# Regrouping two small matrix products and their copies in a recurrent attention kernel followed by a feed-forward network

## The chip, the cores and the metric

The kernel runs on one core of a Trainium2 chip. The core has a tensor engine (PE; its weight loads are listed apart as PEld), a vector engine (DVE), a scalar engine (ACT), GpSimd (POOL) and SyncE (SP), each with its own in-order queue, an on-chip memory (SBUF), and the banks that only the tensor engine writes and that DVE and ACT read (PSUM). The metric is the device time of one execution in microseconds. The kernel before takes 617.74 us, the median of three runs (617.41 to 618.44).

## The reference

Two blocks follow each other. The first is a gated linear recurrence over 4 batches, 8 heads, 768 positions, 48 features per head; the second is a two-layer network with a per-column leaky rectifier over the 3072 tokens, from 384 to 2048 and back.

```python
f = 1.0 / (1.0 + np.exp(-f_logit))
state = np.zeros((B, H, D, D), dtype=np.float32)
for t in range(S):
    state = f[:, :, t, :, None] * state + np.einsum('bhd,bhde->bhde', k[:, :, t], v[:, :, t])
    y[:, :, t] = np.einsum('bhd,bhde->bhe', q[:, :, t], state)
...
h = x @ w_in
g = np.maximum(h, 0.0) + alpha * np.minimum(h, 0.0)
return (g @ w_out).astype(np.float32)
```

Everything is float32.

## The kernel before

**Steps.** The sequence is cut into six chunks of 128 positions and the batches into two pairs. One chunk of one pair is a step, so there are twelve steps, counted 0 to 11 here; a step has the chunk number `c` (0 in steps 0 and 1) and the pair number `bp`. Each step passes through four generators: `prepare` (P in the order strings, and Q for the next step's), `carry` (O), `attend` (S) and `network` (n, which belongs to the step before). Each `yield` ends one piece.

**What a step computes.** `prepare` loads f, q, k and v and forms, on DVE, products of gates with queries and keys at several block sizes; near its end DVE transposes the keys (`kt`), and sixteen transfers on SP's queue (line 427) put them together as `ksn`. `attend` forms the scores within blocks of 32: for each of the two batches of the pair (u = 0, 1) the matmul groups `raw` (line 520) and `qu` (line 535), which DVE copies under masks into `ad` (lines 526 and 541), and which ACT then copies into the score matrix `A` ("score copies", line 563, four for each batch). `carry` forms the scores between the two halves of a 64-chunk, `off` (line 444, "off-diagonal"), which ACT copies into `A` (line 462, four copies), and the increments of the state, `pd` (line 484, "state products"), which DVE adds to the state in `moved` (lines 494 and 498). `attend` then multiplies `A` with values and state, `py` (line 574), and ACT copies it out (`y`, line 583); ten transfers transpose it into `xT`, the network's input.

**The network.** Eight net tiles `ph` (line 618) per step; ACT forms `neg` from each (line 623) and DVE the `gate` (line 625), and after every fourth tile DVE makes sums `S` of gates (line 702). The second layer is done in seven products (`pa`, `pb`, `pc`, `pd`, `pa` and `pc` again, `pe`, line 657). ACT copies the first part of `pa` (line 668, shown as Csum), and DVE adds products up (line 661). The tile name `pd` occurs twice: at line 484 it is the state product, at line 657 the network's.

**Order.** PE, DVE and ACT run their instructions in the order in which the generators are advanced, which is written out in the strings `FIRST` (steps 0 to 3) and `USUAL` (line 37); a number repeats a letter. In a usual step PE's queue reads: raw and qu of batch 0, net tiles 0 and 1, raw and qu of batch 1, net tile 2, off, net tile 3, pd, net tiles 4 to 7, pa, pb, py, pc, pd, pa, pc, pe. On ACT, the copies `us` (line 314, from the queries) of the next step, then the copy of `pa`, then the eight score copies, then `y`.

**PSUM.** `raw`, `qu`, `off`, `pd` and `py` share two places of two banks each (`pair`); a place is handed to the next tile that asks, and that tile waits for the readers of the tile before. The net's tiles and products use four other banks.

Of the kernel before, what the change touches and what calls it, by code (L numbers as in the profile page):

```python
# [8 lines left out]
F32 = mybir.dt.float32  # L9
# [9 lines left out]
DB = 32  # L19
MASKED = (1, 0)  # L20

U = 2
CH = 64
NC2 = C // CH
# [6 lines left out]
FIRST = (  # L31
# [4 lines left out]
)  # L36
USUAL = "S n2 S n O n O n Q n3 Q n Q S3 n Q S n Q n Q n"

def flat(first, usual, steps=12):
    out = []  # L40
# [18 lines left out]
def kernel(  # L59
# [30 lines left out]
    nc = tc.nc  # L90
    B, NC, _, HP, _ = qT.shape
    DM = v.shape[-1]
    H = 2 * HP
    D = DM // H
# [4 lines left out]
    W = U * HP * C  # L99
    GC = W // CH  # L100
    G = W // DB
    NJ = C // DB
# [13 lines left out]
    work = ctx.enter_context(tc.tile_pool(name="work", bufs=2))  # L116
# [5 lines left out]
    def pair(name):  # L122
        return psa.tile([128, 2, 512], F32, tag="pair", name=name)
# [14 lines left out]
    vs = []  # L138
# [24 lines left out]
    for m in range(1, NB):  # L163
        lo = UO[m] + (4 if m == 1 else 0)
        n = NB - m
# [4 lines left out]
    for half in range(2):  # L170
        for m in range(1, NQ):
            n = NQ - m
# [75 lines left out]
    def rows(par):  # L248
        return slice(64 * par, 64 * par + D)
# [4 lines left out]
    def halves(cc):  # L254

        return slice(CH * cc, CH * cc + CH), slice(CH * (1 - cc), CH * (1 - cc) + D)
# [175 lines left out]
    def carry(bp, c, x):  # L432

        i = f"{bp}_{c}"
        q3, ks, kh, f64 = (x[n] for n in ("q3", "ks", "kh", "f64"))
        off = pair(f"off_{i}")
        for u in range(U):
            for hp in range(HP):
                for cc in range(NC2):
                    g = (u * HP + hp) * NC2 + cc  # L440
                    o = (u * HP + hp) * DB
                    for par in range(2):
                        r_ = rows(par)
                        nc.tensor.matmul(off[CH * cc:CH * cc + DB, par, o:o + DB],
                                         lhsT=kh[r_, g], rhs=q3[r_, g, 2], start=True, stop=True)
        if not c:
            for u in range(U):
                for hp in range(HP):
                    for j in range(NJ):
                        g = (u * HP + hp) * NJ + j  # L450
                        o = U * HP * DB + (u * HP + hp) * 16
                        for par in range(2):
                            r_ = rows(par)
                            nc.tensor.matmul(off[DB * j:DB * (j + 1), par, o:o + 16], lhsT=x["k16"][r_, g],
                                             rhs=x["q16"][r_, g], start=True, stop=True)
            for u in range(U):
                o = U * HP * DB + u * HP * 16
                nc.scalar.copy(ad[:, u, :, :, 16:DB], off[:, :, o:o + HP * 16].rearrange("p r (h t) -> p r h t", h=HP))
        for cc in range(NC2):
            s_ = slice(CH * cc, CH * cc + DB)  # L460
            for par in range(2):
                nc.scalar.copy(A[s_, :, par * HP:(par + 1) * HP, CH * cc + DB:CH * (cc + 1)],
                               off[s_, par, 0:U * HP * DB].rearrange("p (u h t) -> p u h t", u=U, h=HP))


        if not c:
            pk = pair(f"pk_{i}")
            for u in range(U):
                for hp in range(HP):
                    a = (u * HP + hp) * NC2  # L470
                    nc.tensor.transpose(pk[:, u, hp * 128:(hp + 1) * 128], ks[:, a:a + 2].rearrange("p c s t -> p (c s t)"), ident)
            ksn = x["ksn"] = work.tile([128, U, HP * 128], F32, tag="ksn", name=f"ksn_{i}", bufs=1)
            for u in range(U):
                nc.scalar.copy(ksn[:, u], pk[:, u])
        yield
        pd = pair(f"pd_{i}")
        ksn = x["ksn"]
        for u in range(U):
            for hp in range(HP):
                for cc in range(NC2):  # L480
                    for par in range(2):
                        o = (u * HP + hp) * D
                        s_ = halves(cc)[0]
                        nc.tensor.matmul(pd[rows(par), cc, o:o + D],
                                         lhsT=ksn[s_, u, hp * 128 + 64 * par:hp * 128 + 64 * par + D],
                                         rhs=vs[bp][s_, cc, u, (2 * hp + par) * D:(2 * hp + par + 1) * D], start=True, stop=True)

        def moved(cc):

            of, to = halves(cc)[1], halves(1 - cc)[1]  # L490
            was, then = (vs[bp][p, a, :, 0:DM].rearrange("p u (h e) -> p u h e", e=D)
                         for p, a in ((of, cc), (to, 1 - cc)))
            if c or cc:
                nc.vector.tensor_tensor(then, was, f64[of].unsqueeze(3).broadcast_to((D, U, H, D)), ALU.mult)
            for par in range(2):
                now = pd[rows(par), cc, 0:U * HP * D].rearrange("p (u h e) -> p u h e", u=U, e=D)
                if c or cc:
                    nc.vector.tensor_tensor(then[:, :, par:H:2], then[:, :, par:H:2], now, ALU.add)
                else:
                    nc.scalar.copy(then[:, :, par:H:2], now)  # L500

        x["moved"] = moved
        moved(0)
        yield

    def attend(bp, c, x):

        i = f"{bp}_{c}"
# [2 lines left out]

        QL, QS = (UW, UW) if c else (VW, C)
        for u in range(U):
            raw = pair(f"raw{u}_{i}")
            for hp in range(HP):
                for j in range(NJ):
                    g = (u * HP + hp) * NJ + j
                    for par in range(2):
                        r_ = rows(par)
                        nc.tensor.matmul(raw[DB * j:DB * (j + 1), par, hp * C:hp * C + QW],  # L520
                                         lhsT=k[r_, g * DB:(g + 1) * DB], rhs=qd[r_, g], start=True, stop=True)
            adu = ad[:, u].rearrange("p r h (i t) -> p (r h) i t", t=4)
            rv = raw.rearrange("p r (h x) -> p (r h) x", h=HP)
            for d in range(4):
                n = 4 - d
                nc.vector.copy_predicated(  # L526
                    adu[:, :, :, d:4], mraw[:, d, :, d:4].bitcast(I32).unsqueeze(1).broadcast_to((128, H, NB, n)),
                    rv[:, :, QO[d]:QO[d] + NB * n].rearrange("p h (i t) -> p h i t", t=n))
            qu = pair(f"qu{u}_{i}")
            for hp in range(HP):  # L530
                for j in range(NJ):
                    g = (u * HP + hp) * NJ + j
                    for par in range(2):
                        r_ = rows(par)
                        nc.tensor.matmul(qu[DB * j:DB * (j + 1), par, hp * QS + 4:hp * QS + QL],  # L535
                                         lhsT=k4[r_, g * DB:(g + 1) * DB], rhs=us[r_, g, 4:QL], start=True, stop=True)
            if c:
                for m in range(1, NB):
                    lo = UO[m] + (4 if m == 1 else 0)
                    n = DB - 4 * m  # L540
                    nc.vector.copy_predicated(  # L541
                        ad[:, u, :, :, 4 * m:DB],
                        mquad[:, lo:lo + n].bitcast(I32).unsqueeze(1).unsqueeze(1).broadcast_to((128, 2, HP, n)),
                        qu[:, :, 0:HP * UW].rearrange("p r (h x) -> p r h x", h=HP)[:, :, :, lo:lo + n])
            else:
                qv = qu.rearrange("p r (h x) -> p (r h) x", h=HP)
                adh = ad[:, u].rearrange("p r h (a t) -> p (r h) a t", a=2)
                for m in range(1, NQ):
                    n = 4 * (NQ - m)
                    lo = 4 if m == 1 else VO[m]  # L550
                    hi = lo + (DB - 4 if m == 1 else 2 * n)
                    to, of, by = ad[:, u].rearrange("p r h t -> p (r h) t")[:, :, 4:DB], qv[:, :, lo:hi], mhalf[:, lo:hi]
                    by = by.bitcast(I32).unsqueeze(1).broadcast_to((128, H, hi - lo))
                    if m > 1:
                        to = adh[:, :, :, 4 * m:16]
                        of, by = (t.rearrange("p h (a t) -> p h a t", a=2) for t in (of, by))
                    nc.vector.copy_predicated(to, by, of)
            yield
# [175 lines left out]
    with tc.manual_schedule(engines={mybir.EngineType.PE, mybir.EngineType.DVE, mybir.EngineType.Activation}):  # L734
# [3 lines left out]
        for n, step in enumerate(steps):  # L738
            x = {}
# [59 lines left out]
```

## Time and profile before

| | |
|---|---|
| median of three runs | 617.74 us |
| profiled execution, span from the first to the last instruction | 616.6 us |
| PE busy | 587.9 us (95%) |
| DVE busy | 496.0 us (80%) |
| ACT busy | 245.7 us (40%) |
| mean granted TensorE clock | 0.997 |
| step 5, from its raw group to the next step's (242.85 to 290.27) | 47.42 us, PE busy 47.32, DVE 41.27, ACT 17.77 |
| groups of step 5 on PEld | off 0.65 us, pd 0.81, py 1.13 and 0.90, net tile 2 2.46 |

A row of the timeline gives the start from the span's beginning, the duration, the engine, the line, the operation, what is written and read, the shape, and how many instructions were merged (fp32 matmuls appear twice each); a bracket at its end gives the idle time of the engine just before, and what ended it ("issue" when the profile shows nothing that it waited for). Rows of PEld, the weight loads, tell best when PE could go on. SPq rows are issues of transfers, not the transfers themselves.

### The profile page before, as it was taken

What the parts mean: (1) busy time and instruction counts of PE and PEld (TensorE: products, weight loads), DVE (VectorE), ACT (ScalarE), POOL (GpSimd) and SP (SyncE); (2) the same over time, 40 slices, a digit from 0 to 9 for tenths busy, and PEclk for the clock granted to TensorE, in tenths of its full rate; (3) what the DMA queues carried; (4) which work ended last, traced back from release to release, by engine and by line L of the source; (5) the groups of instructions that cost most, each with busy time, mean ns of one, the idle gap of its engine ahead of it and who ended that gap; (6) DMA issues with size and microseconds to landing.
All of it is one profiled execution on the core that took longest, in us unless ns stands there. A gap on an engine that the chain in (4) does not pass through costs nothing.

```text
span 616.6 us, 19078 instructions
## 1 busy us (share of the span) xinstructions
PE 587.9 (95%) x8220; PEld 525.1 (85%) x8220; DVE 496.0 (80%) x997; ACT 245.7 (40%) x466; POOL 62.8 (10%) x117
## 2 busy tenths in 40 slices
PE   3568999999999999999999999999999999999997
PEld 3457867898899899899889899899889889889997
DVE  7599898899898798798798798798898889762251
ACT  5687852441641361262261261352352343223110
POOL 9120010001010011001001001001001000000000
PEclk9998999999999999999999999999999999999999
DMA  9965532014414214214313313413413301201000
GB/s 302 368 236 180 161 86 54 35 37 120 89 31 75 70 39 105 67 35 98 78 34 93 83 35 90 86 35 87 89 35 86 89 2 27 55 1 27 27 1 26
DMA packets 68116, 50.43 MB, mean 82 GB/s; under 512 B 47168, under 2 KB 60608, under 8 KB 68032
## 3 DMA queue, kind: packets, MB, share of 16 engines
q1 hardware_dynamic: 56656, 25.01, 15.6%
q0 software_dynamic: 6864, 22.35, 13.0%
q10 hardware_dynamic: 4512, 1.85, 1.7%
q8 instruction: 65, 1.06, 0.7%
q14 instruction: 19, 0.16, 0.1%
HBM read 36.21 MB, written 4.72 MB: 66 GB/s over the span
## 4 chain that ended last, share of the span: by engine, by line
PE 67%; DVE 19%; ACT 9%; issue 4%; DMA 1%; ACTq 0%; SPq 0%; DVEq 0%
PE ph L618 27%; PE pc L657 9%; PE pa L657 6%; PE pd L657 5%; PE pe L657 4%; PE po L638 3%; PE raw L520 3%; DVE gate L625 3%; PE qu L535 3%; ACT A L563 3%; DVE S L702 3%; DVE qd L287 3%; PE py L574 3%; ACT us L314 2%; PE pb L657 2%
## 5 line engine op out<-in xcount | busy, mean ns | idle before, releaser
L618 PE MATMUL ph<-xT,w_in_sb 128*128 128x256 f32 x1152 | 261.2, 383 | 0.7 <-DVE Csum L661 0.7
L618 PEld LDWEIGHTS ph<-xT,w_in_sb 128*128 128x128 f32 x1152 | 215.9, 190 | 33.2 <-issue 2.4
L623 ACT ACTIVATE neg<-ph 128x512 f32<-128x512 f32 x96 | 57.2, 596 | 198.2 <-PE ph L618 157.1
L625 DVE SCALAR_TENSOR_TENSOR gate<-neg,om,ph 128x256 f32<-128x256 f32 x192 | 82.3, 477 | 52.3 <-ACT neg L623 52.1
L657 PE MATMUL pc<-t,S 128*128 128x192 f32 x352 | 61.7, 329 | 0.0
L657 PE MATMUL pa<-w_out_sb,gate 128*128 128x192 f32 x352 | 61.3, 327 | 0.1
L657 PEld LDWEIGHTS pa<-w_out_sb,gate 128*128 128x128 f32 x352 | 57.9, 190 | 1.0 <-DVE gate L625 0.4
L657 PEld LDWEIGHTS pc<-t,S 128*128 128x128 f32 x352 | 57.3, 190 | 0.6
L526 DVE COPY_PREDICATED ad<-mraw,raw 128x256 f32<-128x256 int32 (+1 forms) x96 | 42.4, 441 | 10.7 <-PE raw L520 8.2
L541 DVE COPY_PREDICATED ad<-mquad,qu 128x224 f32<-128x224 int32 (+6 forms) x140 | 42.0, 300 | 6.2
L419 ACT COPY A<-q 48x512 f32<-48x512 f32 x44 | 27.2, 617 | 36.4 <-DVE q L368 35.9
L563 ACT COPY A<-ad 32x256 f32<-32x256 f32 x96 | 38.5, 401 | 1.4
L330 DVE TENSOR_TENSOR us<-us,fs 128x768 f32<-128x768 f32 (+5 forms) x60 | 36.7, 612 | 0.0
L678 ACT ACTIVATE o<-pa 128x192 f32<-128x192 f32 x11 | 3.6, 330 | 75.2 <-PE pa L657 65.4
L661 DVE SCALAR_TENSOR_TENSOR Csum<-pc,Csum 128x192 f32<-128x192 f32 x22 | 7.8, 356 | 29.8 <-PE pc L657 29.6
L574 PEld LDWEIGHTS py<-A,vs 128*64 128x64 f32 x768 | 25.7, 145 | 6.1 <-issue 2.8
L702 DVE TENSOR_TENSOR S<-gate 128x512 f32<-128x512 f32 x44 | 30.3, 688 | 0.8
L574 PE MATMUL py<-A,vs 128*64 128x64 f32 x768 | 28.7, 232 | 1.9 <-ACT vs L500 0.9
L657 PE MATMUL pd<-w_out_sb,S 128*128 128x192 f32 x176 | 30.4, 326 | 0.0
L657 PE MATMUL pb<-t,gate 128*128 128x192 f32 x176 | 30.4, 326 | 0.0
L657 PE MATMUL pe<-w_out_sb,S 128*128 128x192 f32 x176 | 30.4, 326 | 0.0
L520 PEld LDWEIGHTS raw<-qd,k 48*32 48x32 f32 x1536 | 18.5, 109 | 13.5 <-issue 11.1
(101 smaller groups left out, 744.3 us busy)
## 6 DMA issues: line engine op xcount, KB each, us to landing
w_out_raw<-in_w_out SPq DMA_DIRECT2D x8, 767.8 KB, 5.3
w_in_raw<-in_w_in SPq DMA_DIRECT2D x8, 767.2 KB, 12.1
q<-in_qT POOLq DMA_DIRECT2D x11, 512.0 KB, 4.2
f<-in_fT POOLq DMA_DIRECT2D x11, 512.0 KB, 4.5
k<-in_kT POOLq DMA_DIRECT2D x11, 512.0 KB, 4.8
out<-o SPq DMA_DIRECT2D x24, 192.0 KB, 3.0
vs<-in_v POOLq DMA_DIRECT2D x22, 192.0 KB, 4.8
ksn<-kt SPq DMA_DIRECT2D x80, 32.0 KB, 2.0
```

Source lines behind the costliest of these rows:

```text
L330: nc.vector.tensor_tensor(us[:, :, UO[m]:UO[m] + 4 * n].rearrange("p g (i r) -> p g i r", r=4), us[:, :, skip:skip + 4 * n].rearrange("p g ...
L419: nc.scalar.copy(A[halves(cc)[1], :, par * HP:(par + 1) * HP, CH * cc:CH * (cc + 1)], q3[rows(par)].rearrange("p (u h c) s t -> p u h c (s ...
L520: nc.tensor.matmul(raw[DB * j:DB * (j + 1), par, hp * C:hp * C + QW], lhsT=k[r_, g * DB:(g + 1) * DB], rhs=qd[r_, g], start=True, stop=True)
L526: nc.vector.copy_predicated(adu[:, :, :, d:4], mraw[:, d, :, d:4].bitcast(I32).unsqueeze(1).broadcast_to((128, H, NB, n)), rv[:, :, QO[d]: ...
L541: nc.vector.copy_predicated(ad[:, u, :, :, 4 * m:DB], mquad[:, lo:lo + n].bitcast(I32).unsqueeze(1).unsqueeze(1).broadcast_to((128, 2, HP, ...
L563: nc.scalar.copy(A[s_, u, :, s_], ad[s_, u].rearrange("p r h t -> p (r h) t"))
L574: nc.tensor.matmul(py[64 * par:64 * par + 64, u, o:o + CH], lhsT=vs[bp][:, cc, u, hd * D:hd * D + 64], rhs=A[:, u, par * HP + hp, CH * cc: ...
L618: nc.tensor.matmul(ph[:, j * T:(j + 1) * T], lhsT=w_in_sb[:, kt, m * 128:(m + 1) * 128], rhs=xT[:, kt], start=(kt == 0 and j == 0), stop=( ...
L623: nc.scalar.activation(neg, phv, AF.Relu, scale=-1.0)
L625: nc.vector.scalar_tensor_tensor(gate[:, m % NH, m // NH], neg[:, j], om[:, m:m + 1], phv[:, j], ALU.mult, ALU.add)
L657: nc.tensor.matmul(to[:, 0:DH], lhsT=of(f), rhs=by(f), start=(f == 0 and not more), stop=(f == NH - 1), skip_group_check=True)
L702: nc.vector.tensor_tensor(to, x_, y_, op)
```

## The change

Three edits. First, for steps with c above 0 `carry` is one piece instead of two: the state products are issued first, and the off products and their copies directly behind them; the order strings lose one O, and the place of the remaining one is that of the former second, before net tile 4. For c = 0 the order stays as it was. Second, in `attend` the place for the second batch's `qu` is asked for before that of its `raw`. Third, in `USUAL` the two pieces of score copies stand one network piece earlier: behind the second piece of the next step's `prepare` and ahead of pa and pb, instead of behind them.

```diff
-        "n S P n2 S W n W n O Q n3 O S Q n S Q n Q S2 Q n3",
-        "S n3 P S Q S n O n O n4 Q S Q S Q n S Q n Q n2",
+        "n S P n2 S W n W n Q n3 O S Q n S Q n Q S2 Q n3",
+        "S n3 P S Q S n2 O n4 Q S Q S Q n S Q n Q n2",
 )
-USUAL = "S n2 S n O n O n Q n3 Q n Q S3 n Q S n Q n Q n"
+USUAL = "S n2 S n2 O n Q n3 Q S2 n Q S n Q S n Q n Q n"
...
+        def increments():
+            pd = pair(f"pd_{i}")
+            ksn = x["ksn"]
...
+            x["moved"] = lambda cc: moved(pd, cc)
+
+        def across():
+            q3, kh = x["q3"], x["kh"]
+            off = pair(f"off_{i}")
...
+        if c:
+            increments()
+            across()
+        else:
+            ks = x["ks"]
+            across()
+            pk = pair(f"pk_{i}")
...
+            yield
+            increments()
+        x["moved"](0)
         yield
...
         for u in range(U):
+            if u:
+                qu = pair(f"qu{u}_{i}")
             raw = pair(f"raw{u}_{i}")
...
-            qu = pair(f"qu{u}_{i}")
+            if not u:
+                qu = pair(f"qu{u}_{i}")
```

The bodies of `increments` and `across` are the matmul loops and copies that stood in `carry` before.

More of the change, by code (lines that the diff above doesn't have):

```diff
@@ L434, in carry @@
         i = f"{bp}_{c}"
[L435 to L486, printed above, removed]
@@ L488, in moved @@
-        def moved(cc):
+        f64 = x["f64"]
+        def moved(pd, cc):
             of, to = halves(cc)[1], halves(1 - cc)[1]
@@ L500, in moved @@
                     nc.scalar.copy(then[:, :, par:H:2], now)
-        x["moved"] = moved
-        moved(0)
+        def increments():
+            pd = pair(f"pd_{i}")
+            ksn = x["ksn"]
+            for u in range(U):
+                for hp in range(HP):
+                    for cc in range(NC2):
+                        for par in range(2):
+                            o = (u * HP + hp) * D
+                            s_ = halves(cc)[0]
+                            nc.tensor.matmul(pd[rows(par), cc, o:o + D],
+                                             lhsT=ksn[s_, u, hp * 128 + 64 * par:hp * 128 + 64 * par + D],
+                                             rhs=vs[bp][s_, cc, u, (2 * hp + par) * D:(2 * hp + par + 1) * D],
+                                             start=True, stop=True)
+            x["moved"] = lambda cc: moved(pd, cc)
@@ new lines, in across @@
+        def across():
+            q3, kh = x["q3"], x["kh"]
+            off = pair(f"off_{i}")
+            for u in range(U):
+                for hp in range(HP):
+                    for cc in range(NC2):
+                        g = (u * HP + hp) * NC2 + cc
+                        o = (u * HP + hp) * DB
+                        for par in range(2):
+                            r_ = rows(par)
+                            nc.tensor.matmul(off[CH * cc:CH * cc + DB, par, o:o + DB],
+                                             lhsT=kh[r_, g], rhs=q3[r_, g, 2], start=True, stop=True)
+            if not c:
+                for u in range(U):
+                    for hp in range(HP):
+                        for j in range(NJ):
+                            g = (u * HP + hp) * NJ + j
+                            o = U * HP * DB + (u * HP + hp) * 16
+                            for par in range(2):
+                                r_ = rows(par)
+                                nc.tensor.matmul(off[DB * j:DB * (j + 1), par, o:o + 16], lhsT=x["k16"][r_, g],
+                                                 rhs=x["q16"][r_, g], start=True, stop=True)
+                for u in range(U):
+                    o = U * HP * DB + u * HP * 16
+                    nc.scalar.copy(ad[:, u, :, :, 16:DB], off[:, :, o:o + HP * 16].rearrange("p r (h t) -> p r h t", h=HP))
+            for cc in range(NC2):
+                s_ = slice(CH * cc, CH * cc + DB)
+                for par in range(2):
+                    nc.scalar.copy(A[s_, :, par * HP:(par + 1) * HP, CH * cc + DB:CH * (cc + 1)],
+                                   off[s_, par, 0:U * HP * DB].rearrange("p (u h t) -> p u h t", u=U, h=HP))
@@ new lines, in carry @@
+        if c:
[5 more added lines that the diff above has]
+            pk = pair(f"pk_{i}")
+            for u in range(U):
+                for hp in range(HP):
+                    a = (u * HP + hp) * NC2
+                    nc.tensor.transpose(pk[:, u, hp * 128:(hp + 1) * 128], ks[:, a:a + 2].rearrange("p c s t -> p (c s t)"), ident)
+            ksn = x["ksn"] = work.tile([128, U, HP * 128], F32, tag="ksn", name=f"ksn_{i}", bufs=1)
+            for u in range(U):
+                nc.scalar.copy(ksn[:, u], pk[:, u])
+            yield
+            increments()
```

## The prediction

> **What bounds the kernel now.** I read the page first, for the engine that is full.
>
> ```profile
> span 616.6 us, 19078 instructions
> PE 587.9 (95%) x8220; PEld 525.1 (85%) x8220; DVE 496.0 (80%) x997; ACT 245.7 (40%) x466; POOL 62.8 (10%) x117
> ...
> PEclk9998999999999999999999999999999999999999
> ```
>
> TensorE is full from about 45 us on at a full granted clock; a step in the middle (from one raw group to the next step's, 242.85 to 290.27) lasts 47.42 us, of which PE is busy 47.32. So time is won or lost only where the tensor queue pauses. The pauses show in the timeline of the weight loads (PEld), whose bracket gives the idle time before each group. Step 5, the first line being the end of net tile 2:
>
> ```profile
> 251.85 2.46 PEld L618 LDWEIGHTS ph<-xT,w_in_sb 128*128 128x128 f32 x12 [0.17 <-issue]
> 254.64 0.65 PEld L444 LDWEIGHTS off<-q,kh 48*32 48x32 f32 x64 [0.33 <-issue]
> 255.33 2.46 PEld L618 LDWEIGHTS ph<-xT,w_in_sb 128*128 128x128 f32 x12
> 258.12 0.81 PEld L484 LDWEIGHTS pd<-vs,ksn 64*48 64x48 f32 x64 [0.33 <-issue]
> 258.98 10.23 PEld L618 LDWEIGHTS ph<-xT,w_in_sb 128*128 128x128 f32 x48
> ...
> 274.74 1.13 PEld L574 LDWEIGHTS py<-A,vs 128*64 128x64 f32 x36 [0.23 <-issue]
> 276.10 0.90 PEld L574 LDWEIGHTS py<-A,vs 128*64 128x64 f32 x28 [0.24 <-ACT A L563]
> ```
>
> The reader should see three pauses. Going from a net tile to the off group costs 0.33 us, to the pd group again 0.33; going back costs 0.04 (off ends 255.29, net starts 255.33) and 0.05. And py stops for 0.24 in its second half, for the score copies. ScalarE's timeline shows why:
>
> ```profile
> 270.53 2.19 ACT L314 COPY us<-qd 128x256 f32<-128x256 f32 x4
> 272.46 0.41 ACT L668 ACTIVATE Csum<-pa 128x192 f32<-128x192 f32 x1
> 272.74 3.32 ACT L563 COPY A<-ad 32x256 f32<-32x256 f32 x8
> ```
>
> The eight score copies end at 276.06, and py resumes at 276.10. VectorE's timeline gives what ScalarE hangs on:
>
> ```profile
> 258.90 0.87 DVE L625 SCALAR_TENSOR_TENSOR gate<-neg,om,ph 128x256 f32<-128x256 f32 x2 [2.30 <-ACT neg L623]
> ...
> 280.05 0.36 DVE L661 SCALAR_TENSOR_TENSOR Csum<-pc,Csum 128x192 f32<-128x192 f32 x1 [1.42 <-PE pc L657]
> ```
>
> VectorE has no idle row from gate 3 (258.90) until 278.63, so that chain, which feeds the last neg, the us copies and the score copies, starts when net tile 3 is finished.
>
> **The change, part by part** (steps counted 0 to 11; orders read from the two programs' instruction lists).
>
> *Grouping.* In steps 2 to 11 the off group leaves its place before a net tile and stands behind pd. VectorE's, SyncE's and GpSimd's instructions keep their order. Per step, before: 254.31 to 255.33 for off (1.02) and 257.79 to 258.98 for pd (1.19), 2.21 together. After: 0.33 + 0.81 (pd) + a gap pd to off + 0.65 (off) + 0.04. The gap has no row: pd and off have different shapes (64*48, 48*32). Bounds: raw to qu, same shape, where at 203.37 the second's loads start 0.07 before the first's end; and net to off, 0.33. I take 0.06, by the nearest rows: a small group left for another shape cost 0.04 and 0.05, because its last matmul is short (205 ns against the net's 379). Sum 1.89, saved 0.32. Step 2 gains nothing: there the pa group waits 0.38 for a gate on VectorE, which is busy throughout from 115.6 and not sped up. Nine steps: 2.88 us. With the bounds the grouping saves 9 x 0.45 = 4.05 or 9 x 0.05 = 0.45.
>
> [...] The rows say that the price lies on leaving the long matmuls, so I keep 2.88.
>
> *New waits.* off now waits for the last qu copy of the second batch (ends 255.83; off would start at 257.97, 2.1 us spare), pd for the last raw copy, earlier still. Behind off on PE stands net tile 4, and its four copies on ScalarE (1.27 us) now stand ahead of neg 4: they run from about 258.8 to 260.1, net tile 4 is ready at about 261.6. Free; without that cover each late microsecond would delay a step by one. neg 3 is no longer behind the off copies and net tile 3 ends 1.02 earlier, so VectorE's chain moves up by about 1 us.
>
> *pd comes 1.02 us earlier, the transfers that it needs do not.* pd waits for 16 ksn transfers from SyncE. Twelve of them are issued behind an output store that hangs on the step's first VectorE sums, so their time is tied to the step's start. The row of the last issue, and the transfer view asked for that one issue (size, then us from issue to landing), give when it lands; steps 6 and 7 are the late ones:
>
> ```profile
> 301.68 0.61 SPq L427 DMA_DIRECT2D ksn<-kt  x1
> ```
>
> ```profile
> ksn<-kt SPq DMA_DIRECT2D x1, 16.0 KB, 3.4
> ```
>
> ```profile
> 348.33 0.61 SPq L427 DMA_DIRECT2D ksn<-kt  x1
> ```
>
> ```profile
> ksn<-kt SPq DMA_DIRECT2D x1, 16.0 KB, 4.7
> ```
>
> ```profile
> 352.80 1.10 PEld L484 LDWEIGHTS pd<-vs,ksn 64*48 64x48 f32 x64 [0.33 <-issue]
> ```
>
> Step 6 lands at 305.06 (301.68 + 3.38, shown as 3.4); pd would start at 305.42 - 1.02 = 304.40: 0.66 late, price 0.68. Step 7 lands at 353.04 (pd lasts 1.10 instead of 0.81 already); pd would start at 351.78, end where it ends now, and off's 0.7 follows behind: price 1.03 against the saving above. The same sum leaves 0.26 spare in step 3, 4.9 in step 4, 0.6, 0.14, 0.15, 0.5 and 3.2 in steps 5, 8, 9, 10 and 11. In this draw 1.71 us are lost. Bounds: 0 (all on time) and 8 x 1.03 = 8.24 (steps 4 to 11 all like step 7). I take 1.71, the rows themselves.
>
> *Score copies.* The label says ahead of query copies. In the order of ScalarE they stay behind the us copies (made from the queries) and pass only the copy of pa (Csum, 0.41 us, 0.27 until the next row) in steps 4 to 11. With VectorE's chain earlier, neg 7 becomes bound by net tile 7 (from 270.03 to about 269.4), so the score copies end near 275.2 and py, starting at 274.41, needs them at 275.5: the stall goes. Its size: the py groups of steps 4 to 11 last 2.30, 2.26, 2.32, 2.01, 2.28, 2.33, 2.30 and 2.15 us; step 2, undisturbed, has 1.95. Sum of the excess 2.35. Bounds: 0 and 2.35; I take 2.35, as 0.3 us are spare. Step 3's order keeps the copies where they are, and its 0.5 stays. The copy of pa comes some 3 us later, at 275.6; its readers are the sum on VectorE at 280.05 and pa's second half at 282.38, which gains a wait on it. Free by over 4 us.
>
> *Second-score banks first.* The banks given to every score tile, and the waits, are the same with and without this edit. Nothing.
>
> **Sum.** 2.88 + 2.35 - 1.71 = 3.52 us off the profiled execution's 616.57 (span). The median, 617.74, is 1.17 above that span; I take the difference as constant: **614.2 us**.
>
> **Rivals.** Least difference that a measurement of this kernel tells: 0.2%, 1.24 us.
>
> - *The ksn transfers are on time* (hidden anyway). For it: six of eight were in time. Against: three had 0.26 or less to spare. 617.74 - 5.23 = 612.5.
> - *The third switch costs as much as the first.* For it: no row of pd to off. Against: every exit from a short matmul cost 0.04 to 0.06. Grouping saves 0.45: 617.74 - 0.45 - 2.35 + 1.71 = 616.65, no change.
> - *The change doesn't do what it says*: the score copies, still behind the us copies, gain only the 0.27 us of the copy they pass, while PE gains 0.32, and py stalls on. Needs VectorE's chain not to move. 617.74 - 2.88 + 1.71 = 616.6, no change.
> - *Slower: pd stands waiting for ksn in nearly every step, with off and the net behind it.* For it: a group that waits now holds up 0.7 us of off as well, and the key transfer that runs beside ksn is untouched. Against: only two of eight were late enough. It decides from (5.23 + 1.24)/8 = 0.81 us a step; at 1.03 in all eight, 617.74 + 3.0 = 620.75.
>
> **Numbers.** The forecast 0.58 (own range 612.6 to 615.9: ksn losses from nearly none to twice the draw), ksn on time 0.18, dear third switch 0.07, py stalls on 0.07, slower 0.10. Faster is the first two, 0.76; same the next two, 0.14; slower 0.10. Range: down to 611.3, which is no ksn loss and a gap at its lower bound (612.5 - 9 x 0.13); up to 617.6, which takes in both no-change cases and ksn losses three times the draw (617.74 - 5.23 + 5.13), and leaves out the slower case.
>
> **What would show it.** In the weight loads' timeline: one 0.33 pause ahead of pd, off directly behind it with 0.1 or less between; no row of py waiting for A in steps 4 to 11; gate 3 on VectorE about 1 us earlier against the raw group. pd rows longer than 0.81 us are late ksn; their excess is the loss. The prediction is wrong if the gap behind pd is 0.2 or more, if most pd rows exceed 1.3 us, or if VectorE's chain does not move and py keeps its second row.

## The result, and the profile after

The changed kernel takes 614.81 us, the median of four runs (614.14 to 615.66); four runs of the kernel before beside them gave 618.07. The ratio is 0.9953, with a 95% interval of 0.9939 to 0.9967: faster by 0.47%, some 2.9 us. The forecast was 614.2.

The head of the page of the changed kernel, whose profiled execution took 614.73 us:

```profile
span 612.9 us, 19072 instructions
...
PE 585.0 (95%) x8220; PEld 525.4 (86%) x8220; DVE 496.7 (81%) x997; ACT 246.5 (40%) x466; POOL 62.8 (10%) x117
...
PEclk9999999999999999999999999999999999999999
```

The span is 3.7 us shorter with the same 8220 matmuls, and PE is still full. Step 5 in the timeline of the weight loads (start, duration, what is loaded, and in brackets the idle time before), to be held against the same step before:

```profile
250.60 5.05 PEld L631 LDWEIGHTS ph<-xT,w_in_sb 128*128 128x128 f32 x24 [0.17 <-issue]
255.98 0.81 PEld L460 LDWEIGHTS pd<-vs,ksn 64*48 64x48 f32 x64 [0.33 <-issue]
256.84 0.65 PEld L476 LDWEIGHTS off<-q,kh 48*32 48x32 f32 x64
257.53 10.23 PEld L631 LDWEIGHTS ph<-xT,w_in_sb 128*128 128x128 f32 x48
...
273.29 1.95 PEld L587 LDWEIGHTS py<-A,vs 128*64 128x64 f32 x64 [0.23 <-ACT A L576]
```

One pause of 0.33 is left, ahead of pd; off follows pd after 0.05 (255.98 + 0.81 to 256.84). py is one row of 1.95 us, where it had been two with 0.24 between them. (Its bracket names a score copy now, but the idle time ahead of it is the 0.23 that it was.) ScalarE's timeline of the same step:

```profile
257.64 1.27 ACT L494 COPY A<-off 32x256 f32<-32x256 f32 x4 [0.91 <-PE off L476]
...
268.74 2.20 ACT L314 COPY us<-qd 128x256 f32<-128x256 f32 x4
270.70 3.36 ACT L576 COPY A<-ad 32x256 f32<-32x256 f32 x8
274.09 0.33 ACT L681 ACTIVATE Csum<-pa 128x192 f32<-128x192 f32 x1
```

The score copies end at 274.06. py's second half is reached 1.13 us after 273.29 (the length of its first row before), at 274.42: 0.36 to spare. VectorE's gate 3 stands here:

```profile
256.77 0.87 DVE L638 SCALAR_TENSOR_TENSOR gate<-neg,om,ph 128x256 f32<-128x256 f32 x2 [1.40 <-ACT neg L636]
```

That is 15.13 us behind the step's first raw load (241.64); before it was 16.05 (258.90 against 242.85). Not everything was gained. Two pd rows are longer than 0.81, in steps 9 and 10:

```profile
444.10 1.19 PEld L460 LDWEIGHTS pd<-vs,ksn 64*48 64x48 f32 x64 [0.33 <-issue]
...
491.39 0.87 PEld L460 LDWEIGHTS pd<-vs,ksn 64*48 64x48 f32 x64 [0.33 <-issue]
```

And in step 6 PE stops in the middle of net tile 4, waiting for nothing that the profile shows:

```profile
304.42 1.38 PEld L631 LDWEIGHTS ph<-xT,w_in_sb 128*128 128x128 f32 x7
306.59 2.56 PEld L631 LDWEIGHTS ph<-xT,w_in_sb 128*128 128x128 f32 x12 [0.80 <-issue]
```

Step lengths of the two profiled executions, from one step's first raw load to the next one's (the last column runs to the end of the span):

| step | 2 | 3 | 4 | 5 | 6 | 7 | 8 | 9 | 10 | 11 and end |
|---|---|---|---|---|---|---|---|---|---|---|
| before | 44.63 | 48.23 | 47.22 | 47.42 | 47.37 | 47.35 | 47.31 | 47.36 | 47.48 | 89.44 |
| after | 44.65 | 48.14 | 46.65 | 46.86 | 47.66 | 46.85 | 46.84 | 47.15 | 46.98 | 88.97 |

Together 3.05 us less, over single executions of the two kernels. Another 0.58 of this pair's difference lies ahead of step 2 (its start, 102.77 and 102.19), which in the kernels below lies between 101.6 and 104.8 and is not put down to the change. Steps 4, 5, 7, 8, 10 and 11 gain about 0.5 each; step 2 nothing; step 3 0.09; step 9 loses 0.38 of its gain to late keys; step 6 is longer than before, by the pause.

### The profile page after: what moved, and what is told of

The parts are those of the page before. It is cut to its first block, busy times and chain, and to the rows that moved or that the text cites. A ratio compares the mean times of both kernels' runs of the same rounds, so it can differ in the third digit from the quotient of the medians.

```text
span 612.9 us, 19072 instructions
## 1 busy us (share of the span) xinstructions
PE 585.0 (95%) x8220; PEld 525.4 (86%) x8220; DVE 496.7 (81%) x997; ACT 246.5 (40%) x466; POOL 62.8 (10%) x117
## 4 chain that ended last, share of the span: by engine, by line
PE 86%; DVE 9%; ACT 2%; issue 1%; DMA 1%; SPq 0%; ACTq 0%; DVEq 0%
PE ph L631 39%; PE pc L670 9%; PE pa L670 9%; PE pd L670 5%; PE pe L670 4%; PE pb L670 4%; PE py L587 3%; PE po L651 3%; PE raw L532 3%; PE qu L548 3%; PE pd L460 1%; PE off L476 1%; DVE ad L538 1%; DVE qd L287 1%; DVE gate L638 1%
## 5 line engine op out<-in xcount | busy, mean ns | idle before, releaser
L631 PE MATMUL ph<-xT,w_in_sb 128*128 128x256 f32 x1152 | 258.0, 382 | 1.4 <-DVE Csum L674 0.8
L532 PE MATMUL raw<-qd,k 48*32 48x80 f32 x1536 | 24.1, 243 | 6.5 <-issue 3.4
L266 POOL DMA_DIRECT2D k<-in_kT x11 | 8.0, 728 | 207.4 <-PE raw L532 207.4
```

What stands on the lines that cost most here:

```text
L631: nc.tensor.matmul(ph[:, j * T:(j + 1) * T], lhsT=w_in_sb[:, kt, m * 128:(m + 1) * 128], rhs=xT[:, kt], start=(kt == 0 and j == 0), stop=( ...
```

## The experiments

All kernels below start from the kernel after unless said otherwise. "n" in an order string is one piece of the network, "O" the carry, "S" a piece of attend, "Q" one of the next step's prepare.

### Each edit alone

The grouping alone, with the score copies where they had been:

```diff
-USUAL = "S n2 S n2 O n Q n3 Q S2 n Q S n Q S n Q n Q n"
+USUAL = "S n2 S n2 O n Q n3 Q n Q S3 n Q S n Q n Q n"
```

> The grouping without the moved score copies. In the changed kernel's weight loads a net tile that follows another net tile lasts 2.59 us with its gap, one that follows a small group 2.46 to 2.50; so a break costs 0.33 + 0.04 - 0.13 = 0.24 at most, not 0.37, and the grouping should save about 0.20 us a step (9 steps: 1.8), not 0.32 (2.9). Theory 'chain': net tile 3 a whole off group earlier moves VectorE's chain and with it the score copies by about 0.5 us, which by itself ends py's stall (0.3 us a step, 2.35 in all): py rows of 1.95 us nearly everywhere, about 614.3 to 615. Theory 'order': the stall goes only because the score copies pass the copy of pa: py rows stay at 2.2 to 2.3, about 616.2.

Measured: 615.1 us, ratio 0.9952 [0.9940, 0.9964]. The score copies alone, in the kernel before:

```diff
-USUAL = "S n2 S n O n O n Q n3 Q n Q S3 n Q S n Q n Q n"
+USUAL = "S n2 S n O n O n Q n3 Q S2 n Q S n Q S n Q n Q n"
```

> The kernel before with only the score copies moved ahead of the copy of pa in the usual steps. Theory 'chain': VectorE's chain does not move, the copies come 0.27 us earlier by the copy that they pass, and 0.31 of stall shrink to about 0.05 (py rows about 2.0): 2.0 us off, about 616.0. Theory 'order': py rows of 1.95 everywhere, 2.35 off, 615.7. If the copies wait for something else, such as the last masked copies, py keeps 2.2 to 2.3 and the time stays at 618.

Measured: 616.25 us, ratio 0.9964 [0.9952, 0.9976]. Both edits together save 0.47%, the one alone 0.48%, the other 0.36%: they are not a sum. The ACT and PEld timelines say why. First step 5 of the grouping alone:

```profile
271.52 0.33 ACT L681 ACTIVATE Csum<-pa 128x192 f32<-128x192 f32 x1
271.75 3.32 ACT L576 COPY A<-ad 32x256 f32<-32x256 f32 x8
```

```profile
274.01 2.00 PEld L587 LDWEIGHTS py<-A,vs 128*64 128x64 f32 x64 [0.23 <-issue]
```

The copies still stand behind the copy of pa and end at 275.07, and py's second half is due only at 275.14. py lasts 2.00, 0.05 over. Then step 5 of the copies alone:

```profile
270.94 3.35 ACT L563 COPY A<-ad 32x256 f32<-32x256 f32 x8
```

```profile
273.18 2.06 PEld L574 LDWEIGHTS py<-A,vs 128*64 128x64 f32 x64 [0.23 <-issue]
```

Here they end at 274.29, with py's half due at 274.31; py lasts 2.06, 0.11 over. The stall of 0.3 us is cut to 0.05 or 0.11 by either edit, by the grouping because VectorE's chain moves up (gate 3 at 15.16 us into step 5, 16.05 before), by the new order because the copies pass the copy of pa. Over steps 4 to 11 about 0.6 and 0.7 of the 2.35 us remain; with the grouping alone py of step 11 lasts 2.15, as before. What the grouping adds to the copies alone is 616.25 - 614.81 = 1.4 us (by the ratios 0.0011, 0.7 us).

The second edit undone (the place of the second batch's `qu` asked for after that of `raw`):

```diff
         for u in range(U):
-            if u:
-                qu = pair(f"qu{u}_{i}")
             raw = pair(f"raw{u}_{i}")
...
-            if not u:
-                qu = pair(f"qu{u}_{i}")
+            qu = pair(f"qu{u}_{i}")
```

> The changed kernel without the edit that asks for the second batch's qu place first. Theory 'it does nothing': the tensor queue's rows, banks and waits are those of the changed kernel, time 614.8 within 0.7. Rival: the place order matters, then raw or qu rows of the second batch lengthen or gain a pause.

Measured: 615.0 us, ratio 0.9945 [0.9929, 0.9960]. The same as the kernel after; the edit does nothing.

### The order within the group

```diff
         if c:
-            increments()
             across()
+            increments()
```

> Grouped as in the changed kernel, but off ahead of pd. pd then starts 0.7 us later, and the ksn transfers, late by 0.38 and 0.06 in two steps of the changed kernel's profile, are in time everywhere: every pd row 0.81 us. Theory 'late transfers cost': 0.3 to 0.5 us less than the changed kernel's 614.8, about 614.4. Theory 'the order within the group matters in itself' (shape switch off to pd dearer than pd to off): a gap of 0.2 or more between the two and a loss of over 1.3 us against the changed kernel.

Measured: 621.07 us, ratio 1.0047 [1.0035, 1.0059], 6 us slower than the kernel after and slower than the kernel before. Both expectations fell. The weight loads of step 5:

```profile
258.45 0.65 PEld L476 LDWEIGHTS off<-q,kh 48*32 48x32 f32 x64 [0.33 <-issue]
259.31 1.49 PEld L460 LDWEIGHTS pd<-vs,ksn 64*48 64x48 f32 x64 [0.21 <-PE off L476]
```

off to pd costs 0.21 where pd to off costs 0.05, and pd itself takes 1.38 to 1.52 in steps 2 to 11 instead of 0.81. It is not the keys: in steps 4 and 11 the last of them lands over 4 us before pd, and pd lasts 1.49 there too. Pd waits for many transfers, and the trace shows nine semaphore waits for it on a row of PE's load sequencer (PEldq), of which the first starts 3.96 us ahead of pd's first load in the kernel after (252.02 against 255.98). First those of step 5 in the kernel after (shortest, median and longest in ns, start of the first and of the last), then those here:

```profile
L460 PEldq EVENT_SEMAPHORE  x9: 51/51/2822, 252.0 to 255.8; - x9
```

```profile
L460 PEldq EVENT_SEMAPHORE  x9: 51/51/51, 259.0 to 259.9; - x9
```

In the kernel after they lie between 252.02 and 255.85, while net tiles 2 and 3 occupy PE, and are all done before pd's first load at 255.98; even the one of 2.82 us, which waits for a key transfer, costs nothing: pd lasts 0.81. Here all are of 51 ns, they start 0.105 to 0.17 us apart, and they lie between 258.95 and 259.98: the first starts 0.50 us behind off's first load (258.45), and six of the nine fall behind pd's first load (259.31). So the reading is that nine waits of this kind are hidden behind a net tile (matmuls of 379 ns, the median in step 5 of the kernel after) and not behind off (193 ns).

That reading was tested by splitting pd. Its first 8 of 32 products, which carry all the waits, are issued behind the net tile, then off, then the other 24:

```diff
         if c:
-            increments()
+            pd = increments(range(2))
             across()
+            increments(range(2, U * HP), pd)
```

> The eight matmuls of pd that carry all its waits, then off, then pd's other 24 matmuls, in one group. With off ahead of pd the pd group lasted 1.49 us instead of 0.81, with a pause after each pair of its first loads. Theory 'the semaphore waits are exposed' (each takes the queue 0.05 us and more, and only a long net tile ahead of them hides them): here they stand behind the net tile again, the whole group lasts about 1.55 to 1.7 us as in the changed kernel (1.51), steps of 46.9 us. Theory 'pd behind off is slow by its shape': the 24 later matmuls spread out, steps of 47.4 us or more.

```profile
258.69 0.27 PEld L463 LDWEIGHTS pd<-vs,ksn 64*48 64x48 f32 x16 [0.33 <-issue]
259.01 0.65 PEld L480 LDWEIGHTS off<-q,kh 48*32 48x32 f32 x64
259.70 0.63 PEld L463 LDWEIGHTS pd<-vs,ksn 64*48 64x48 f32 x48
```

The part of pd that stands behind off now takes 0.63 for 24 products, and the whole 1.64 us (258.69 to 260.33), against 2.35 in the kernel with off first (258.45 to 260.80) and 1.51 in the kernel after. So it is neither the shape nor the change from off to pd that costs (0.04 here, 259.66 to 259.70); the waits directly behind off are what the slow kernel has and this one has not. The one run took 618.46 us; its step 2 began at 104.84, 2.65 later than in the kernel after. Its steps 4, 5, 8 and 9 last 46.79 to 46.93; step 6 lasts 47.43, with a pause of 0.46 in net tile 4, and step 7 47.79, with keys 0.87 late. So the total says nothing against this.

### What one break costs

Net tile 4 put between pd and off again, in steps 3 to 11; in step 2 it is pd that moves, one net tile ahead:

```diff
-        "n S P n2 S W n W n Q n3 O S Q n S Q n Q S2 Q n3",
-        "S n3 P S Q S n2 O n4 Q S Q S Q n S Q n Q n2",
+        "n S P n2 S W n W n Q n2 O n O S Q n S Q n Q S2 Q n3",
+        "S n3 P S Q S n2 O n O n3 Q S Q S Q n S Q n Q n2",
 )
-USUAL = "S n2 S n2 O n Q n3 Q S2 n Q S n Q S n Q n Q n"
+USUAL = "S n2 S n2 O n O Q n3 Q S2 n Q S n Q S n Q n Q n"
...
         if c:
             increments()
+            x["moved"](0)
+            yield
             across()
+            yield
+            return
```

> The changed kernel with net tile 4 put between pd and off again in steps 2 to 11 (pd stays where it is, off comes one net tile later); score copies as changed. This measures what one break of the net's tiles costs. Theory 'a net tile behind a net tile is slower' (0.03 + 2.56 against 0.04 + 2.45): each undisturbed step is 0.20 longer than the changed kernel's 46.85, 47.05 us. Theory 'the whole 0.33 and more is saved' (the forecast's 0.32): 47.17 us.

Measured: 617.87 us, ratio 1.0000 [0.9981, 1.0018]. The total fits the prediction's price, but it does not come from there: steps 4 to 6 and 8 to 10 lasted 46.86 to 47.1, 0.1 to 0.2 above undisturbed steps of the kernel after, and step 7, with keys 0.58 late, 47.60. Step 2 took 48.59 instead of 44.65, of which step 3 gave 0.8 back. In step 2 the group stands directly ahead of pa. VectorE's additions to the state (128.67 to 130.84) now stand ahead of the last gates, pa waited 2.68 us for one of these, and the granted clock was 0.50 from 131.9 to 135.3 us. So it was run again with step 2 left as it is in the kernel after (only the piece in `carry` is shown; step 3 and the usual steps have the order strings above):

```diff
         if c:
             increments()
+            if (c, bp) != (1, 0):
+                x["moved"](0)
+                yield
             across()
...
```

> The kernel after, with net tile 4 put between the state products and the off-diagonal ones again in steps 3 to 11 (nine steps); step 2 stays as in the kernel after, and the orders of VectorE, SyncE and GpSimd stay in all steps. It measures the price of one break. Theory of the prediction (a break costs 0.32 us): 9 x 0.32 = 2.9 us above the kernel after's 614.8, 617.7. Rival, from the rows of the kernel after (a net tile that comes directly behind a net tile takes back 0.13 of what the pause costs, so a break costs 0.1 to 0.2): 0.9 to 1.8 us above, 615.7 to 616.6, and steps 4 to 10 of 46.85 to 47.0 us where no transfer is late.

Measured: 616.26 us, ratio 0.9965 [0.9953, 0.9977]: 1.45 us above the kernel after, 0.7 by the ratios; for nine breaks 0.08 to 0.16 us each, late keys included (0.88 here in step 7, 0.44 in the kernel after). A price of 0.32 would have given a ratio of 1.000 (0.9953 + 2.88/618). Steps 4 and 5 last 46.85 and 47.00, 0.20 and 0.14 longer. The loads of step 5:

```profile
256.63 0.81 PEld L460 LDWEIGHTS pd<-vs,ksn 64*48 64x48 f32 x64 [0.33 <-issue]
257.50 2.46 PEld L638 LDWEIGHTS ph<-xT,w_in_sb 128*128 128x128 f32 x12
260.29 0.65 PEld L476 LDWEIGHTS off<-q,kh 48*32 48x32 f32 x64 [0.33 <-issue]
```

The second pause of 0.33 is back. But net tile 4, which follows a small group, takes 2.46 us and ends so early that part of the pause is paid back: net tiles that follow a net tile take 0.03 + 2.56 (in the kernel after, net tile 3 runs from 253.08 to 255.65 inside the merged row), those behind a small group 0.04 + 2.46. Of each pause saved, 0.13 us (0.03 + 2.56 against 2.46) is lost again to the next net tile.

### The group one net tile earlier

```diff
-USUAL = "S n2 S n2 O n Q n3 Q S2 n Q S n Q S n Q n Q n"
+USUAL = "S n2 S n O n2 Q n3 Q S2 n Q S n Q S n Q n Q n"
```

> The changed kernel with the group one net tile earlier in the usual steps (4 to 11), behind net tile 2. The last ksn transfer lands 13.1 to 14.3 us after the step's first raw group, in steps 5 to 10, and the group would start at about 11.7. Theory 'late transfers cost their lateness' (the mechanism of the forecast's slower case): pd rows of 2.2 to 3.2 us in steps 5 to 10, these steps at 48.5 to 49.5 instead of 46.85, some 11 to 15 us in all, about 626 to 629. Rival: the transfers land earlier when pd comes earlier, or the wait is made good later in the step: under 619.

Measured: 637.72 us in one run, beyond what was expected. This is the slower rival, made to happen: pd now stands 2.5 us earlier and waits for ksn in steps 5 to 10. The loads of step 6:

```profile
305.15 0.16 PEld L460 LDWEIGHTS pd<-vs,ksn 64*48 64x48 f32 x2 [0.33 <-issue]
306.66 1.35 PEld L460 LDWEIGHTS pd<-vs,ksn 64*48 64x48 f32 x62 [1.35 <-issue]
308.06 0.85 PEld L476 LDWEIGHTS off<-q,kh 48*32 48x32 f32 x64
```

And the busy times of PE, PEld, DVE, ACT and POOL in stretches of 2 us behind that wait, followed by the granted clock:

```profile
308.00:310.00 2.00, 2.00 (x78) 1.70 (x70) 1.30 (x3) 0.89 (x3) 0.00 (x0) 0.56 0.03 8
310.00:312.00 2.00, 2.00 (x7) 1.63 (x6) 0.00 (x0) 0.37 (x2) 0.00 (x0) 0.58 0.03 8
312.00:314.00 2.00, 2.00 (x11) 1.77 (x10) 0.13 (x1) 0.60 (x1) 0.00 (x0) 1.00 0.00 0
```

The wait costs 1.35 us, and then the clock is halved for about 3.4 us, (0.44 + 0.42) x 2 / 0.5. The pd rows of steps 5 to 10 add up to 3.48, 2.86, 4.92, 2.84, 3.02 and 3.36 us; the last key transfer lands 1.8 to 3.7 us after pd's first load. The steps last 49.5 to 51.9, so 2.5 to 5 us are lost in each. The pause of 1.35 us ahead of this half clock has small matmuls on both sides of it.

The length of a pause is not all that counts. Step 10 has one of 1.94 us and no half clock behind it:

```profile
510.75 1.25 PEld L460 LDWEIGHTS pd<-vs,ksn 64*48 64x48 f32 x62 [1.94 <-DMA out<-o]
```

```profile
512.00:514.00 2.00, 2.00 (x79) 1.78 (x71) 1.10 (x2) 1.13 (x4) 0.00 (x0) 1.00 0.03 8
```

The half clock of step 6 begins at about 308.2 (2 x 0.44 us of the stretch from 308 on were lost, at half the clock), 1.6 us behind the end of its pause. What decides whether one follows is not shown: no run changed the length or the time of one pause by itself.

Steps 4 and 11, whose keys are in time, lose 0.65 and 0.67 us to something else: off starts 0.62 and 0.64 us behind pd.

```profile
208.77 0.66 PEld L476 LDWEIGHTS off<-q,kh 48*32 48x32 f32 x64 [0.62 <-PE pd L460]
```

The profile names pd, but VectorE's last copy of the second batch's `qu` ends at 208.65: it is the wait of off on these copies, for which the prediction counted 2.1 us to spare in its own place.

### The group one net tile later

Here the group has more time for its keys; step 3 gets the later place too, and the early score copies that the change left out there.

```diff
-        "S n3 P S Q S n2 O n4 Q S Q S Q n S Q n Q n2",
+        "S n3 P S Q S n3 O n2 Q S n Q S Q n S Q n Q n2",
 )
-USUAL = "S n2 S n2 O n Q n3 Q S2 n Q S n Q S n Q n Q n"
+USUAL = "S n2 S n3 O Q n3 Q S2 n Q S n Q S n Q n Q n"
```

> The changed kernel with the group one net tile later in steps 3 to 11, behind net tile 4, and in step 3 the us copies and score copies ahead of the copy of pa, as the usual steps have them. Theory 'late transfers cost': pd starts 16.9 us into the step, no ksn transfer is late, every pd row 0.81; the 0.1 to 1.0 us that the grouped runs lost are kept, and py of step 3 lasts 1.95 instead of 2.45: about 614.2 against 614.8 to 615.0. Rival: off's copies, now behind neg 4 and ahead of the sigmoid on ScalarE, push VectorE's chain back and the py or pa rows grow: 615 or more.

Measured: 613.35 us, ratio 0.9913 [0.9895, 0.9931]: the fastest of all kernels here. No pd row of steps 1 to 11 is longer than 0.81; step 3 lasts 47.62 instead of 48.14, with py in one row:

```profile
180.16 1.95 PEld L587 LDWEIGHTS py<-A,vs 128*64 128x64 f32 x64 [0.23 <-issue]
```

Steps 4 to 10 lie between 46.69 and 46.92. To split the two parts, the first of the two lines was changed alone:

> The kernel after, with the order of step 3 alone changed: the joined group behind net tile 4 instead of net tile 3, and the score copies ahead of pa and pb as in the later steps; steps 4 to 11 as in the kernel after. Theory: the kernel with both orders changed took 613.35 because py's second row in step 3 (0.5 us) goes and because ksn is in time in the steps after; the first part alone gives 0.5, so 614.3, and the late rows of pd in steps 7 to 10 remain. Rival: the gain of that kernel was all in step 3 and the steps behind it are as long as before: 613.4.

(In step 3 the group had stood behind net tile 4 and stands behind net tile 5 here; the expectation counts one too low.) Measured: 615.06 us, ratio 0.9938 [0.9922, 0.9953]. Against the kernel after the interval leaves open whether it is faster. The steps are clearer: step 3 lasts 47.53, 0.61 less, and of the steps behind it none is systematically shorter (46.67, 46.88, 47.80, 46.92, 46.83, 46.78, 47.07). The rival, that all of the gain was in step 3, does not fit the steps of the two profiled executions: the kernel with both parts is shorter behind step 3 too. But the rest of the gain was not mostly late keys, as the theory had it. From step 4 on the profiled execution with both parts is 1.6 us shorter; 1.0 of that is step 6 (46.79 against 47.80), where this kernel has the pause of the kernel after, of 1.07 us, in the same net tile, and the kernel with both parts has none. Late keys are 0.32 of it (steps 7 and 10). With one profile of each and ratios whose intervals just touch (0.9895 to 0.9931 and 0.9922 to 0.9953), this split is likely, not shown.

## Why the prediction was right

The total was right, 614.81 against 614.2, and the three signs that the prediction named came. That it was right to 0.6 us is partly luck: two of its terms were too large by more than 1 us, one a gain and one a loss, and a pause that it did not foresee took 0.8.

- *Grouping, forecast 2.88.* The place of the pauses was right, the size was not. The gap behind pd, where the shape changes, is 0.05 (taken: 0.06); that it is small because pd's last matmul is short (205 ns) was the author's estimate, and no run tests it. But from net tile 2's start to net tile 4's start it was 7.13 us before (251.85 to 258.98) and is 6.93 now: 0.20 a step, 1.8 in nine. The step that failed is the sum of 2.21 against 1.89 over the two small groups alone: it left out that net tile 3, now directly behind a net tile, takes 0.13 longer. The kernels with the group broken up again put a break at 0.1 to 0.2 too.
- *Step 2 gains nothing.* Right: 44.65 after 44.63.
- *py's stalls, forecast 2.35.* Right: all py rows of steps 4 to 11 last 1.95, and step 3's stall of 0.42 remains. The cause was half told. The prediction let the stall go on if VectorE's chain did not move; in fact either the earlier chain or the passing of pa's copy alone takes away most of it (all but 0.6 or 0.7).
- *Late ksn, forecast 1.71 lost.* The place was half right, the size was not. In the profile after 0.44 is lost, in steps 9 and 10 and not in 6 and 7, and the 0.29 that step 7 lost before is gone: 0.15 net. The step that failed is the tie of the transfers to the step's start with the landings of one execution: pd stands 0.93 us earlier against the step's start, not 1.02 (in step 5 14.34 behind the first raw load, before 15.27), and the landings differ from run to run. With pd in the same place, step 7's pd row lasts 1.83 in the grouping alone, 1.81 with the second edit undone, 1.69 and 1.39 with the group broken up, and 0.96 with step 3 alone changed. That is the step that the prediction named, but not in every execution, and never the 2.12 that its sum amounts to (351.78 to 353.90). In step 6 none of them is late. All late rows together cost 0.32 to 1.02 us in these kernels and the kernel after; the forecast's would have cost 2.00 (1.71 and the 0.29 of before).
- *New waits and VectorE's chain.* Right: the off copies end at 258.91, neg 4 starts only at 260.48, the copy of pa at 274.09; the chain is 0.92 earlier. neg 7 comes 0.57 earlier in the step (26.61 against 27.18), near the 0.6 forecast.
- *Second-score banks.* Right: nothing.
- *Not foreseen:* the pause of about 0.8 us in step 6.

The sum by the rows of after: 1.8 + 2.35 - 0.44 + 0.29 - 0.77 (step 6's pause) = 3.2, where the steps show 3.05. Of the rivals, keys in time came nearer to this profile (0.15 lost) than the forecast's 1.71, but its 612.5 was missed, since the grouping gave 1.1 less and step 6 paused. The dear third switch (0.33 from pd to off) is excluded by the 0.05, and the change that does nothing by py's single rows. The slower one is a real mechanism: it did not apply in this place, and did 2.5 us earlier, where behind a wait of 1.35 us the clock was halved for about 3.4 us.

## What to carry to other kernels

When the full engine's pauses are counted, measure from a fixed point ahead of the groups to one behind them, long tiles included: part of a pause that is saved may be taken back by the next tile (here 0.13 of 0.33 us). Two edits that end the same stall are not a sum (0.48% and 0.36% here, together 0.47%); see how much is spare after the first. And when the first instructions of a group collect many waits, see what runs ahead of it: in this kernel pd took 0.81 us behind a net tile and 1.49 behind off, and the order of these two alone decided between 0.5% faster and 0.5% slower.

## What the runs showed of the hardware

- In step 5 of the kernel with off first, the nine semaphore waits for pd on PE's load sequencer last 51 ns each and start some 0.11 us apart. pd's row there is 0.68 us longer than in the kernel after (1.49 against 0.81), where net tiles run during these waits, and the gap ahead of it is 0.16 longer than that from pd to off (0.21 against 0.05).
- With the group one net tile earlier, the pause of 1.35 us in step 6 was followed by about 3.4 us at half clock, and the one of 1.94 in step 10 was not. In the kernel first broken up the wait of 2.68 us in step 2 was followed by half a clock from 131.9 to 135.3. The pauses of 0.98 and 1.00 in step 3 of the kernels before and after were not: the clock is 1.00 in the stretches behind them. Earlier, the kernel before has half a clock from 52.0 to 55.4 us, so not a full one throughout from 45 us on, and the kernel after from 44.3 to 47.7.
- A net tile (six 128x256 fp32 products) takes 2.46 us behind a small group (net tile 2 in step 5 of the kernel before) and 2.56 behind another net tile (net tile 3 in step 5 of the kernel after).
- In the kernel after, in the one with the second edit undone and in the one with step 3 alone changed, the weight loads stand still for 0.80, 0.98 and 1.07 us in step 6's net tile 4, once each, and for 0.46 with pd split. In the kernel after an instruction transfer of 16 KB starts at 304.00, 1.8 us ahead of the pause, and takes 1.34 us; in the kernel before one starts at 303.02, with no such pause behind it. What the loads waited for is not shown.
- In the traces of this kernel only PE's rows write the PSUM tiles; no run here shows that DVE and ACT could not. The weight loads do not all start in the program's order: in step 5 of the kernel before, the first load of qu starts at 243.46, ahead of the last one of raw at 243.47.
